# Linformer attention and maxout FFN: q's transposes of six batches moved from TensorE to the DMA crossbar, with early q loads and smaller output stores

## The chip, the cores and the metric

One core of one Trainium2 chip. The metric is device time in microseconds of one execution; most executions agree within 0.3%. Where two kernels are compared, the ratio is the mean time of one kernel's fast runs over that of the other's of the same rounds, so it is not quite the ratio of the medians quoted beside it. Executions over 1.5% slower than the fastest of the same kernel are left out of the means.

## The reference

```python
q, k, v: (8, 8, 1024, 64) f32        # batch, heads, sequence, head dim
E, F:    (64, 1024)                   # project the sequence to 64
k_proj = einsum('ks,bhsd->bhkd', E, k);  v_proj = einsum('ks,bhsd->bhkd', F, v)
attn   = softmax(q @ k_proj.T / 8) @ v_proj
x      = attn.transpose(0, 2, 1, 3).reshape(8192, 512)
h      = max(x @ w1, x @ w2, x @ w3)   # 512 -> 768
out    = h @ w_out                     # 8192 x 512 f32
```

The code calls the second half `moe`; a *chunk* is 512 tokens of it, and `jt` counts the six 128-wide blocks of the 768 hidden columns. Tokens are independent after the projections: in which order a batch's 1024 tokens pass through the scores and the FFN does not matter, as long as the stores put them back.

## The kernel before

The scores need q with the head dim on the partitions, for two heads at a time: q^T, 128 x 1024 per head pair. Before, q is loaded with tokens on the partitions, two heads are copied side by side (`q_p2`), TensorE transposes 8 blocks of 128x128 against an identity into PSUM, and a copy brings the result to SBUF. A batch has four head pairs.

```python
# in attention(b, pending), after the loads of q, k, v and the k projection
for g in range(NPAIR):                                    # 4 head pairs
    q_p2 = small.tile([P, SI, 2 * D], BF16, name="q_p2", bufs=3)
    peng = nc.vector if (b == 0 or g < 2) else nc.gpsimd
    peng.tensor_copy(out=..., in_=q_t[:, 2 * g:2 * g + 2, :, :]...)          # L135
    qt_ps = ps_s.tile([P, 512], FP32, name="ps_s").bitcast(BF16)
    for si in range(SI):                                  # 8
        nc.tensor.transpose(out=qt_ps[:, si * P:(si + 1) * P],               # L141
                            in_=q_p2[:, si, :], identity=ident)
    qT_sb = small.tile([P, SI, P], BF16, name="qT_sb", bufs=2)
    nc.any.tensor_copy(out=qT_sb, in_=qt_ps...)                              # L147
    for c in range(NCHUNK):                               # 2: scores, exp
        nc.tensor.matmul(out=sc_ps, lhsT=kpT_bd[:, g, :], rhs=qT_sb[:, csl, :], ...)  # L154
        nc.scalar.activation(out=pT_g[:, csl, :], in_=sc_ps, func=AF.Exp, scale=scale)
# ... v projection L172, attention outputs L200, x transposes L220 ...

def moe_chunk(b, xT, ch):                                 # 512 tokens
    o_acc = moe_sb.tile([P, SI_PER_CHUNK, DO], FP32, name="o_acc", bufs=2)
    for jt in range(NJT):                                 # 6
        # 12 matmuls L237 into three ps_m buffers, copy by ACT L245, two max by DVE L247, L248
    for tt in range(SI_PER_CHUNK):                        # 4
        # 6 matmuls L252 into ps_m
        nc.scalar.copy(out=o_acc[:, tt, :], in_=o_ps)                        # L259
    nc.sync.dma_start(out=ov[...], in_=o_acc)             # one store of 1 MB

for b in range(B):
    xTs[b] = attention(b, pending)
    if b == 0: load_weights()
    for args in pending: moe_chunk(*args)                 # the two chunks of batch b-1
    pending = [(b, xTs[b], ch) for ch in range(NCHUNK)]
```

A scheduler orders each engine's instructions when the kernel is built, by program order as the priority and its own estimate of times. On the chip every engine then works through its list in that order: an instruction that waits holds back all behind it on its engine or queue (at 41.57 us VectorE had stood 3.81 us behind one q copy whose load had not landed, with batch 0's outputs behind it).

The softmax here doesn't subtract the row's maximum and nothing guards it: scores larger than these inputs give would overflow.

## Time and profile before

| | before |
|---|---|
| time, median of 4 runs | 467.26 us |
| span of the profiled execution | 465.8 us |
| PE busy, of the span | 93% |
| steady batch (first k projection to the next) | 52.87 us, PE busy in all of it |
| last matmul to the end of the span | 5.36 us |

PE is TensorE, DVE VectorE, ACT ScalarE, POOL GpSimd; SP is the engine that issues the stores and transposes, and SPq its queue. In a line of a timeline come start and length in us, engine, line of the kernel, operation, out<-in and count; in brackets, the idle time before it and what ended that. A "steady batch" here is the attention of batch b woven with the first MoE chunk of batch b-1, then the second chunk alone.

### The profile page before, as it was taken

Reading aid. Unit: us, or ns where it says so; the run is one execution under the profiler, and the core shown is the slowest. Engines: PE = TensorE matmul, PEld = TensorE weight load, DVE = VectorE, ACT = ScalarE, POOL = GpSimd, SP = SyncE. Lnnn points to the kernel's source line nnn. Section 1 sums busy time; section 2 is a strip of 40 time slices with the busy share of each in tenths; the row PEclk is TensorE's granted clock in tenths of the full one; section 3 lists DMA queues with packets and bytes.
Section 4 is the critical chain, followed back from the end, with each engine's and each line's share of the span. In section 5 each row is a group of like instructions: output and inputs, shape, how many; then the busy total and the mean of one; then the engine's idle time right before and its main releaser. Section 6 shows DMA issues by size and latency. Waiting matters only on the chain.

```text
span 465.8 us, 6716 instructions
## 1 busy us (share of the span) xinstructions
PE 434.5 (93%) x2672; PEld 226.5 (49%) x2672; DVE 229.0 (49%) x550; ACT 173.6 (37%) x311; POOL 54.8 (12%) x74
## 2 busy tenths in 40 slices
PE   1474999999999999999999999999999999999995
PEld 1343555455544565455544555445544555444442
DVE  2025575427934376426935377425935277334351
ACT  1142555235432453235432553335432453322322
POOL 7212340004000320005000320001000000000000
PEclk9996999999999999999999999999999999999999
DMA  8999999319720591209820492202020200202102
GB/s 110 207 210 205 206 207 206 117 61 182 121 91 0 139 201 25 90 28 198 137 91 0 128 193 44 91 0 91 2 91 0 91 1 0 92 0 91 54 37 90
DMA packets 30207, 45.78 MB, mean 98 GB/s; under 512 B 1120, under 2 KB 28000, under 8 KB 28128
## 3 DMA queue, kind: packets, MB, share of 16 engines
q0 software_dynamic: 27872, 28.58, 38.1%
q1 hardware_dynamic: 2304, 16.78, 8.7%
q8 instruction: 21, 0.34, 0.3%
q14 instruction: 10, 0.08, 0.0%
HBM read 57.15 MB, written 16.78 MB: 159 GB/s over the span
## 4 chain that ended last, share of the span: by engine, by line
PE 89%; DMA 8%; POOL 1%; DVE 0%; issue 0%; ACT 0%; POOLq 0%
PE ps_m L237 54%; PE ps_m L252 18%; DMA q_t<-in_q_dram 6%; PE ps_s L220 3%; PE ps_s L154 3%; PE ps_s L200 3%; PE ps_s L141 3%; PE ps_s L108 3%; DMA k_t<-in_k_dram 2%; PE ps_s L172 2%; PE ps_s L120 0%; POOL q_t L101 0%; DVE x_sb L210 0%; DVE zinv L209 0%; POOL e_sb L61 0%
## 5 line engine op out<-in xcount | busy, mean ns | idle before, releaser
L237 PE MATMUL ps_m<-xT,w_sb 128*128 128x512 bf16 x1152 | 269.3, 380 | 0.0
L237 PEld LDWEIGHTS <-w_sb 128*128 128x128 bf16 x1152 | 107.6, 98 | 111.5 <-issue 3.1
L247 DVE TENSOR_TENSOR m<-ps_m,h1s 128x512 f32<-128x512 f32 x96 | 66.2, 689 | 112.6 <-PE ps_m L237 112.0
L245 ACT COPY h1s<-ps_m 128x512 f32<-128x512 f32 x96 | 56.3, 587 | 105.0 <-PE ps_m L237 104.1
L252 PE MATMUL ps_m<-wout_sb,hT 128*128 128x512 bf16 x384 | 85.7, 379 | 0.0
L248 DVE TENSOR_TENSOR hT<-ps_m,m 128x512 bf16<-128x512 f32 x96 | 66.0, 688 | 8.0 <-PE ps_m L237 2.0
L259 ACT COPY o_acc<-ps_m 128x512 f32<-128x512 f32 x64 | 37.5, 586 | 71.3 <-PE ps_m L252 71.2
L252 PEld LDWEIGHTS <-hT 128*128 128x128 bf16 x384 | 37.4, 98 | 45.1 <-DVE hT L248 3.5
L225 ACT COPY xT<-ps_s 128x512 bf16<-128x512 bf16 x58 | 34.1, 588 | 60.7 <-PE ps_s L220 60.7
L210 DVE TENSOR_TENSOR x_sb<-ps_s,zinv 128x256 bf16<-128x256 f32 x128 | 48.6, 417 | 0.2
L160 ACT ACTIVATE pT_g<-ps_s 128x512 bf16<-128x512 f32 x64 | 34.8, 596 | 19.9 <-PE ps_s L154 19.9
L220 PE MATMUL ps_s<-ident,x_sb 128*128 128x128 bf16 x256 | 35.1, 225 | 6.3 <-DVE x_sb L210 6.3
L220 PEld LDWEIGHTS <-x_sb 128*128 128x128 bf16 x256 | 21.6, 99 | 25.6 <-DVE x_sb L210 14.2
L101 POOL DMA_DIRECT2D k_t<-in_k_dram x16 | 12.0, 752 | 165.7 <-PE ps_s L108 162.1
L200 PE MATMUL ps_s<-vp_bd,pT_g 128*128 128x130 bf16 x256 | 30.3, 227 | 0.5 <-DVE vp_bd L185 0.5
L147 DVE COPY qT_sb<-ps_s 128x1024 bf16<-128x1024 bf16 x31 | 21.4, 692 | 17.4 <-PE ps_s L141 17.2
L135 POOL COPY q_p<-q_t 128x1024 bf16<-128x1024 bf16 x14 | 14.6, 1042 | 127.2 <-PE ps_s L141 110.2
L108 PE MATMUL ps_s<-k_t,eT 128*64 128x256 bf16 x128 | 17.5, 292 | 10.6 <-DMA k_t<-in_k_dram 10.6
L154 PE MATMUL ps_s<-qT_sb,kpT_bd 128*128 128x512 bf16 x64 | 20.9, 409 | 3.5 <-DVE qT_sb L147 2.4
L128 DVE COPY kpT_bd<-ps_s 64x256 bf16<-64x256 bf16 x6 | 1.7, 284 | 45.2 <-PE ps_s L120 45.2
L209 DVE RECIPROCAL zinv<-ps_s 128x4 f32<-128x4 f32 x128 | 17.8, 171 | 8.0 <-PE ps_s L200 7.8
L141 PE MATMUL ps_s<-ident,q_p 128*128 128x128 bf16 x256 | 21.3, 231 | 0.0
(39 smaller groups left out, 150.1 us busy)
## 6 DMA issues: line engine op xcount, KB each, us to landing
out_dram<-o_acc SPq DMA_DIRECT2D x16, 1024.0 KB, 3.9
q_t<-in_q_dram POOLq DMA_DIRECT2D x16, 512.0 KB, 11.4
k_t<-in_k_dram POOLq DMA_DIRECT2D x16, 512.0 KB, 8.8
v_t<-in_v_dram POOLq DMA_DIRECT2D x16, 512.0 KB, 10.7
w_sb<-in_moe_w_dram POOLq DMA_DIRECT2D x3, 768.0 KB, 22.6
wout_sb<-in_moe_w_out_dram POOLq DMA_DIRECT2D x1, 768.0 KB, 25.7
e_sb<-in_E_dram POOLq DMA_DIRECT2D x1, 128.0 KB, 3.0
f_sb<-in_F_dram POOLq DMA_DIRECT2D x1, 128.0 KB, 3.0
```

What stands on the lines that cost most here:

```text
L141: nc.tensor.transpose(out=qt_ps[:, si * P:(si + 1) * P], in_=q_p2[:, si, :], identity=ident,)
L154: nc.tensor.matmul(out=sc_ps, lhsT=kpT_bd[:, g, :], rhs=qT_sb[:, csl, :], start=True, stop=True,)
L160: nc.scalar.activation(out=pT_g[:, csl, :], in_=sc_ps, func=AF.Exp, scale=scale,)
L200: nc.tensor.matmul(out=av_v[:, gg, 0:2 * D + 2], lhsT=pT[g][:, si, :], rhs=vp_bd[:, g, :], start=(gg == 0), stop=(gg == 1),)
L210: nc.vector.tensor_tensor(out=x_sb[:, 4 * u:4 * (u + 1), :].rearrange("p (g par) d -> p g par d", par=2), in0=av_b[:, :, :, 0:D], in1=zinv ...
L220: nc.tensor.transpose(out=xt_v[:, ct, 0:P], in_=x_flat[:, ct * P:(ct + 1) * P], identity=ident,)
L237: nc.tensor.matmul(out=h_ps[i], lhsT=w_sb[i][:, ct, jt * P:(jt + 1) * P], rhs=rhs_x[:, ct, :, :], start=(ct == 0), stop=(ct == NCT - 1),)
L245: nc.scalar.copy(out=h1s, in_=h_ps[0])
L247: nc.vector.tensor_tensor(out=m12, in0=h_ps[1], in1=h1s, op=ALU.max)
L248: nc.vector.tensor_tensor(out=hT[:, jt, :], in0=h_ps[2], in1=m12, op=ALU.max)
L252: nc.tensor.matmul(out=o_ps, lhsT=hT[:, jt, tt * P:(tt + 1) * P], rhs=wout_sb[:, jt, :], start=(jt == 0), stop=(jt == NJT - 1),)
L259: nc.scalar.copy(out=o_acc[:, tt, :], in_=o_ps)
```

## The change

Intent: let the DMA engines transpose q for batches 2 to 7, so that TensorE does only products. q is loaded a batch ahead; its head-pair copies are written to a scratch in HBM, and a transposing DMA reads them back. This also puts tokens in natural order, and the output goes in 128-row stores of 256 KB. The pool of `xT` shrinks from 8 buffers to 6. A *gate* makes the copies for batch b wait for a max in the second MoE chunk of batch b-2. Cut to its core:

```diff
+    PE_BATCHES = {0, 1}                 # these keep the TensorE path
+    def q_prep(b, q_t):
+        for g in range(NPAIR):
+            q_p2 = small.tile([P, SI, 2 * D], BF16, name="q_p2", bufs=4)
+            peng = nc.vector if (g % 2 == 0) else nc.gpsimd
+            cp = peng.tensor_copy(out=..., in_=q_t[...])                       # L106
+            if b - 2 in gate: tc.add_manual_dep(cp.ins, gate[b - 2].ins.name, ...)
+            nc.sync.dma_start(out=qp_dram[b, g]..., in_=q_p2)                   # L115
+            qT = small.tile([P, S], BF16, name="qT", bufs=2 * NPAIR)
+            nc.sync.dma_start(out=qT, in_=qp_dram[b, g], transpose=True)        # L120
   def attention(b, qTs):
-    (loads q, k, v; transposes q on TensorE)
+    (loads k, v; if b in PE_BATCHES: as before, else takes qTs[g])
   def moe_chunk(b, xT, ch):
+            if ch == 1 and jt == 0: gate[b] = hmax
-        (one 1 MB store from o_acc, bufs=2)
+            o_sb = moe_sb.tile([P, DO], FP32, name="o_sb", bufs=3)
+            nc.scalar.copy(out=o_sb, in_=o_ps)                                  # L291
+            nc.sync.dma_start(out=rows, in_=o_sb)      # 128 rows, 256 KB       # L296
   for b in range(B):
     xTs[b] = attention(b, qTs[b])
     if b == 0: load_weights()
+    if b + 1 < B: q_next = q_load(b + 1)
     for args in pending: moe_chunk(*args)
+    if b + 1 < B and b + 1 not in PE_BATCHES: qTs[b + 1] = q_prep(b + 1, q_next)
```

Line numbers change: L141 becomes L171, L147 L177, L154 L185, L108 L137, L237 L266, L252 L283, L259 L291.

More of the change, by code (lines that the diff above doesn't have):

```diff
@@ L45 @@
     NCHUNK = S // CHUNK
-    SI_PER_CHUNK = SI // NCHUNK
+    NTT = S // P
     scale = 1.0 / float(D) ** 0.5
     const = ctx.enter_context(tc.tile_pool(name="const", bufs=1))
-    xt_pool = ctx.enter_context(tc.tile_pool(name="xt_pool", bufs=B))
+    xt_pool = ctx.enter_context(tc.tile_pool(name="xt_pool", bufs=6))
     work = ctx.enter_context(tc.tile_pool(name="work", bufs=2))
@@ L57 @@
     ps_m = ctx.enter_context(tc.tile_pool(name="ps_m", bufs=3, space=bass.MemoryType.PSUM))
+    qp_dram = nc.dram_tensor("qp_scratch", [B, NPAIR, S, 2 * D], BF16, kind="Internal").ap()
     e_sb = const.tile([KP, S], BF16, name="e_sb")
@@ L86, in load_weights, with q_load, attention @@
         nc.gpsimd.dma_start(out=wout_sb, in_=moe_w_out.rearrange("(jt p) m -> p jt m", p=P))
-    out_v = out.rearrange("(b p si) m -> b si p m", p=P, si=SI)
-    def attention(b, pending):
-        def drain(n=1):
-            for _ in range(min(n, len(pending))):
-                moe_chunk(*pending.pop(0))
+    PE_BATCHES = {0, 1}
+    gate = {}
+    def q_load(b):
+        q_t = work.tile([P, H, SI, D], BF16, name="q_t")
+        sv = q[b].rearrange("h (p si) d -> p h si d", si=SI)
+        for hh in range(2):
+            hs = slice(hh * (H // 2), (hh + 1) * (H // 2))
+            nc.gpsimd.dma_start(out=q_t[:, hs], in_=sv[:, hs])
+        return q_t
+    def q_prep(b, q_t):
+        qTs = []
+        for g in range(NPAIR):
+            q_p2 = small.tile([P, SI, 2 * D], BF16, name="q_p2", bufs=4)
+            peng = nc.vector if (g % 2 == 0) else nc.gpsimd
+            cp = peng.tensor_copy(
+                out=q_p2.rearrange("p si (h d) -> p si h d", h=2),
+                in_=q_t[:, 2 * g:2 * g + 2, :, :].rearrange("p h si d -> p si h d"),
+            )
+            if b - 2 in gate:
+                tc.add_manual_dep(
+                    cp.ins, gate[b - 2].ins.name,
+                    mybir.DependencyInfo(mybir.DependencyClass.Sync, mybir.DependencyReason.DATA),
+                    reason="hold q prep")
+            nc.sync.dma_start(
+                out=qp_dram[b, g].rearrange("(p si) c -> p si c", si=SI),
+                in_=q_p2,
+            )
+            qT = small.tile([P, S], BF16, name="qT", bufs=2 * NPAIR)
+            nc.sync.dma_start(out=qT, in_=qp_dram[b, g], transpose=True)
+            qTs.append(qT)
+        return qTs
+    def attention(b, qTs):
         k_t = work.tile([P, H, SI, D], BF16, name="k_t")
         v_t = work.tile([P, H, SI, D], BF16, name="v_t")
-        q_t = work.tile([P, H, SI, D], BF16, name="q_t")
-        for src, dst in ((q[b], q_t), (k[b], k_t), (v[b], v_t)):
+        for src, dst in ((k[b], k_t), (v[b], v_t)):
             sv = src.rearrange("h (p si) d -> p h si d", si=SI)
@@ L132, in attention @@
         for g in range(NPAIR):
-            q_p2 = small.tile([P, SI, 2 * D], BF16, name="q_p2", bufs=3)
-            peng = nc.vector if (b == 0 or g < 2) else nc.gpsimd
-            peng.tensor_copy(
-                out=q_p2.rearrange("p si (h d) -> p si h d", h=2),
-                in_=q_t[:, 2 * g:2 * g + 2, :, :].rearrange("p h si d -> p si h d"),
-            )
-            qt_ps = ps_s.tile([P, 512], FP32, name="ps_s").bitcast(BF16)
-            for si in range(SI):
-                nc.tensor.transpose(
-                    out=qt_ps[:, si * P:(si + 1) * P],
-                    in_=q_p2[:, si, :],
-                    identity=ident,
-                )
-            qT_sb = small.tile([P, SI, P], BF16, name="qT_sb", bufs=2)
-            nc.any.tensor_copy(out=qT_sb, in_=qt_ps.rearrange("a (si p) -> a si p", p=P))
-            pT_g = small.tile([P, SI, P], BF16, name="pT_g", bufs=5)
+            if b in PE_BATCHES:
+                q_p2 = small.tile([P, SI, 2 * D], BF16, name="q_p2", bufs=4)
+                peng = nc.vector if (b == 0 or g < 2) else nc.gpsimd
+                peng.tensor_copy(
+                    out=q_p2.rearrange("p si (h d) -> p si h d", h=2),
+                    in_=qTs[:, 2 * g:2 * g + 2, :, :].rearrange("p h si d -> p si h d"),
+                )
+                qt_ps = ps_s.tile([P, 512], FP32, name="ps_s").bitcast(BF16)
+                for si in range(SI):
+                    nc.tensor.transpose(
+                        out=qt_ps[:, si * P:(si + 1) * P],
+                        in_=q_p2[:, si, :],
+                        identity=ident,
+                    )
+                qT_g = small.tile([P, S], BF16, name="qT", bufs=2 * NPAIR)
+                nc.any.tensor_copy(out=qT_g, in_=qt_ps)
+            else:
+                qT_g = qTs[g]
+            pT_g = small.tile([P, S], BF16, name="pT_g", bufs=5)
             pT.append(pT_g)
@@ L152, in attention @@
                 sc_ps = ps_s.tile([P, 512], FP32, name="ps_s")
-                csl = slice(c * SI_PER_CHUNK, (c + 1) * SI_PER_CHUNK)
+                csl = slice(c * CHUNK, (c + 1) * CHUNK)
                 nc.tensor.matmul(
@@ L156, in attention @@
                     lhsT=kpT_bd[:, g, :],
-                    rhs=qT_sb[:, csl, :],
+                    rhs=qT_g[:, csl],
                     start=True, stop=True,
@@ L160, in attention @@
                 nc.scalar.activation(
-                    out=pT_g[:, csl, :],
+                    out=pT_g[:, csl],
                     in_=sc_ps,
@@ L190, in attention @@
         nc.vector.memset(vp_bd[KP:2 * KP, :, 2 * D + 1:2 * D + 2], 1.0)
-        xT = xt_pool.tile([P, NCT, SI, P], BF16, name="xT")
-        for si in range(SI):
+        xT = xt_pool.tile([P, NCT, S], BF16, name="xT")
+        for tt in range(NTT):
             x_sb = small.tile([P, H, D], BF16, name="x_sb", bufs=3)
@@ L201, in attention @@
                         out=av_v[:, gg, 0:2 * D + 2],
-                        lhsT=pT[g][:, si, :],
+                        lhsT=pT[g][:, tt * P:(tt + 1) * P],
                         rhs=vp_bd[:, g, :],
@@ L224, in attention @@
                 )
-            nc.any.tensor_copy(out=xT[:, :, si, :], in_=xt_v[:, :, 0:P])
+            nc.any.tensor_copy(out=xT[:, :, tt * P:(tt + 1) * P], in_=xt_v[:, :, 0:P])
         return xT
     def moe_chunk(b, xT, ch):
-        if True:
-            o_acc = moe_sb.tile([P, SI_PER_CHUNK, DO], FP32, name="o_acc", bufs=2)
-            hT = moe_sb.tile([P, NJT, CHUNK], BF16, name="hT")
-            rhs_x = xT[:, :, ch * SI_PER_CHUNK:(ch + 1) * SI_PER_CHUNK, :]
-            for jt in range(NJT):
-                h_ps = [ps_m.tile([P, CHUNK], FP32, name="ps_m") for _ in range(3)]
-                for i in range(3):
-                    for ct in range(NCT):
-                        nc.tensor.matmul(
-                            out=h_ps[i],
-                            lhsT=w_sb[i][:, ct, jt * P:(jt + 1) * P],
-                            rhs=rhs_x[:, ct, :, :],
-                            start=(ct == 0),
-                            stop=(ct == NCT - 1),
-                        )
-                h1s = moe_sb.tile([P, CHUNK], FP32, name="h1s", bufs=2)
-                nc.scalar.copy(out=h1s, in_=h_ps[0])
-                m12 = moe_sb.tile([P, CHUNK], FP32, name="m12")
-                nc.vector.tensor_tensor(out=m12, in0=h_ps[1], in1=h1s, op=ALU.max)
-                nc.vector.tensor_tensor(out=hT[:, jt, :], in0=h_ps[2], in1=m12, op=ALU.max)
-            for tt in range(SI_PER_CHUNK):
-                o_ps = ps_m.tile([P, DO], FP32, name="ps_m")
-                for jt in range(NJT):
-                    nc.tensor.matmul(
-                        out=o_ps,
-                        lhsT=hT[:, jt, tt * P:(tt + 1) * P],
-                        rhs=wout_sb[:, jt, :],
-                        start=(jt == 0),
-                        stop=(jt == NJT - 1),
-                    )
-                nc.scalar.copy(out=o_acc[:, tt, :], in_=o_ps)
-            ov = out[b * S:(b + 1) * S, :].rearrange("(p si) m -> p si m", si=SI)
-            nc.sync.dma_start(out=ov[:, ch * SI_PER_CHUNK:(ch + 1) * SI_PER_CHUNK, :], in_=o_acc)
@@ new lines, in moe_chunk @@
+        hT = moe_sb.tile([P, NJT, CHUNK], BF16, name="hT")
+        rhs_x = xT[:, :, ch * CHUNK:(ch + 1) * CHUNK]
+        for jt in range(NJT):
+            h_ps = [ps_m.tile([P, CHUNK], FP32, name="ps_m") for _ in range(3)]
+            for i in range(3):
+                for ct in range(NCT):
+                    nc.tensor.matmul(
+                        out=h_ps[i],
+                        lhsT=w_sb[i][:, ct, jt * P:(jt + 1) * P],
+                        rhs=rhs_x[:, ct, :],
+                        start=(ct == 0),
+                        stop=(ct == NCT - 1),
+                    )
+            h1s = moe_sb.tile([P, CHUNK], FP32, name="h1s", bufs=2)
+            nc.scalar.copy(out=h1s, in_=h_ps[0])
+            m12 = moe_sb.tile([P, CHUNK], FP32, name="m12")
+            nc.vector.tensor_tensor(out=m12, in0=h_ps[1], in1=h1s, op=ALU.max)
+            hmax = nc.vector.tensor_tensor(out=hT[:, jt, :], in0=h_ps[2], in1=m12, op=ALU.max)
+            if ch == 1 and jt == 0:
+                gate[b] = hmax
@@ new lines, in moe_chunk @@
+        for tt in range(CHUNK // P):
+            o_ps = ps_m.tile([P, DO], FP32, name="ps_m")
+            for jt in range(NJT):
+                nc.tensor.matmul(
+                    out=o_ps,
+                    lhsT=hT[:, jt, tt * P:(tt + 1) * P],
+                    rhs=wout_sb[:, jt, :],
+                    start=(jt == 0),
+                    stop=(jt == NJT - 1),
+                )
+            o_sb = moe_sb.tile([P, DO], FP32, name="o_sb", bufs=3)
+            nc.scalar.copy(out=o_sb, in_=o_ps)
+            r0 = b * S + ch * CHUNK + tt * P
+            rows = out[r0:r0 + P, :]
+            if b in PE_BATCHES:
+                rows = out[b * S:(b + 1) * S, :].rearrange("(p si) m -> p si m", si=SI)[:, ch * (CHUNK // P) + tt, :]
+            nc.sync.dma_start(out=rows, in_=o_sb)
@@ L263 @@
+    q_next = q_load(0)
+    qTs = {}
     pending = []
@@ L265 @@
     for b in range(B):
-        xTs[b] = attention(b, pending)
+        if b in PE_BATCHES:
+            qTs[b] = q_next
+        xTs[b] = attention(b, qTs[b])
         if b == 0:
             load_weights()
+        if b + 1 < B:
+            q_next = q_load(b + 1)
         for args in pending:
             moe_chunk(*args)
+        if b + 1 < B and b + 1 not in PE_BATCHES:
+            qTs[b + 1] = q_prep(b + 1, q_next)
         pending = [(b, xTs[b], ch) for ch in range(NCHUNK)]
```

## The prediction

> **What bounds the kernel now.** I read the head of the page first, to see whether one engine is full.
>
> ```profile
> span 465.8 us, 6716 instructions
> PE 434.5 (93%) x2672; PEld 226.5 (49%) x2672; DVE 229.0 (49%) x550; ACT 173.6 (37%) x311; POOL 54.8 (12%) x74
> PE   1474999999999999999999999999999999999995
> DMA  8999999319720591209820492202020200202102
> ```
>
> TensorE is busy 93% of the span. In slices of 11.6 us it is full from the fifth on; before that the DMA engines are full instead. Busy time of pipelined matmuls can flatter, so the chain that ended last comes next:
>
> ```profile
> PE 89%; DMA 8%; POOL 1%; DVE 0%; issue 0%; ACT 0%; POOLq 0%
> PE ps_m L237 54%; PE ps_m L252 18%; DMA q_t<-in_q_dram 6%; PE ps_s L220 3%; PE ps_s L154 3%; PE ps_s L200 3%; PE ps_s L141 3%; PE ps_s L108 3%; DMA k_t<-in_k_dram 2%; PE ps_s L172 2%; PE ps_s L120 0%; POOL q_t L101 0%; DVE x_sb L210 0%; DVE zinv L209 0%; POOL e_sb L61 0%
> ```
>
> The reader is to see two stages: a start on DMA (8%, some 37 us), then nothing but TensorE, with ACT and DVE at nearly none. In the second stage the end moves by exactly the time that is taken out of TensorE's stream. L141, which the change removes for six batches of eight, has 3% of the chain. The view by stretches, cut at the first L108 matmul of each batch, shows how regular this stage is:
>
> ```profile
> 207.49:260.36 52.87, 52.87 (x333) 27.52 (x334) 28.58 (x69) 21.05 (x38) 6.48 (x8) 1.00 0.48 100
> 260.36:313.23 52.87, 52.87 (x333) 27.51 (x334) 28.58 (x69) 21.05 (x38) 6.48 (x8) 1.00 0.48 100
> ```
>
> Columns: length, then PE, PEld, DVE, ACT and POOL busy, granted clock, DMA share, GB/s. A batch takes 52.87 us, PE is busy in all of it at full clock, and the next fullest engine, DVE, has 28.6. What a group of transposes takes of it is read from start to start in PE's timeline, because the modelled ends overlap the next group:
>
> ```profile
> 263.34 0.62 PE L141 MATMUL ps_s<-ident,q_p 128*128 128x128 bf16 x8
> 263.80 1.03 PE L237 MATMUL ps_m<-xT,w_sb 128*128 128x512 bf16 x4
> ...
> 265.17 0.61 PE L141 MATMUL ps_s<-ident,q_p 128*128 128x128 bf16 x8
> 265.62 1.03 PE L237 MATMUL ps_m<-xT,w_sb 128*128 128x512 bf16 x4
> ```
>
> Eight transposes hold the stream for 0.46 and 0.45 us, not for the 0.62 printed as their span; that is 57 ns each.
>
> **What the Trainium skill says.** (1) "TensorE: Matmul & The Clock Gate", section "Wait — 56ns, not 53.3ns?", gives 55.6 ns start to start for warm matmuls of 128 columns; the trace's 57 ns agrees, so the 231 ns mean that the group's row shows for one transpose is latency and must not be multiplied. (2) "DMA: Bandwidth & Descriptors", section "Latency and other measured facts", has 261 GB/s for DMA transposes in one kernel. The trace of before has none, so nothing here confirms it. (3) "VectorE: DVE Perf Modes", section "The three transpose paths", has 1309 ns for one 128x128 through the DMA crossbar; also not shown here. (4) "DMA: Bandwidth & Descriptors", section "Two DMAs through the same engine are not ordered": a DMA that reads what another wrote must wait for its semaphore. So each transposing read waits for its scratch write to land, on SP's queue, which also carries the output stores.
>
> **The change part by part.** *Removed from TensorE:* for batches 2 to 7, 4 groups of 8 transposes. In the batch from 260.36 the groups hold 0.46 + 0.45 + 0.45 + 0.45 = 1.81 us. The chain agrees: L141's share is 2.8% in the longer answer, 13.0 us, and only batches 1 to 7 have it on the chain, so 1.86 us each. Six batches by 1.81 are 10.9 us, all on the path. Their weight loads go with them and lie beside other work.
>
> *Removed from DVE:* 24 copies from PSUM of 0.69 us (row L147: 692 ns), 16.6 us, none of it on the path; five PSUM buffers are also asked for less often. I count nothing.
>
> *Moved:* the head-pair copies of q (0.43 us on DVE, 1.04 us on POOL) go from the attention to the second MoE chunk of an earlier batch, behind the gate. There DVE has 1.10 us idle before each max of the six (its wait rows show 1.10 after hT and before m), and two copies of 0.43 fit. The MoE psum buffers also have slack: hT of one jt ends near 295.83 and its buffer is wanted again at about 296.67. I count 0.
>
> *Added on DMA:* per batch 4 writes of 256 KB to scratch and 4 transposing reads of 256 KB. When do they run, and is there room?
>
> ```profile
> 277.00:281.00 4.00, 4.00 (x37) 2.38 (x35) 3.56 (x14) 1.72 (x3) 0.00 (x0) 1.00 1.25 209
> 285.00:289.00 4.00, 4.00 (x23) 1.95 (x22) 2.74 (x7) 0.92 (x2) 0.00 (x0) 1.00 0.00 0
> 293.00:297.00 4.00, 4.00 (x20) 1.86 (x19) 1.45 (x3) 1.30 (x3) 0.00 (x0) 1.00 0.63 262
> 301.00:305.00 4.00, 4.00 (x20) 1.84 (x19) 1.69 (x4) 1.17 (x2) 0.00 (x0) 1.00 0.00 0
> ```
>
> Same columns. Loads fill the DMA engines until about 282 us; the second chunk (292.35 to 313) leaves them empty apart from one store. The gate (hT of its first jt) would open at about 295.8. Copies end near 298, a write takes about 3 us (estimate: 256 KB against the 3.0 us that a 128 KB load and the 3.9 us that a 1 MB store took to land). A transpose at the skill's 261 GB/s is 1.0 us plus a like latency, about 3 us; four behind each other end near 311 at the latest, and the first near 304. The first score matmul of the next batch came 4.4 us after the batch's start (264.74 against 260.36), so at about 317.6. So the chain is hidden, with 13 us to spare for the first pair. The stores of a chunk come only from 309.4 on, by which time SP should be past its waits. Added on the path: 0.
>
> *Stores:* 64 of 256 KB in place of 16 of 1 MB. Only the last one is on the path.
>
> ```profile
> 460.45 0.59 ACT L259 COPY o_acc<-ps_m 128x512 f32<-128x512 f32 x1 [0.71 <-PE ps_m L252]
> 461.06 0.33 SPq L261 DMA_DIRECT2D out_dram<-o_acc  x1
> ```
>
> From this issue to the end of the span are 4.7 us. In the stretch 293 to 297 one store of 1 MB took 0.63 x 4 = 2.5 us of all 16 engines; a quarter of the bytes takes 0.6, so up to 1.9 us less. I take 1.6. Within a chunk, tiles come 1.30 us apart and there are three output buffers, so the fourth copy wants the first store landed 3 x 1.30 - 0.59 = 3.3 us after it was issued: barely enough for a 256 KB store, and a miss would cost ACT a few tenths that the three MoE psum buffers take up. I count 0.
>
> *Start:* batches 0 and 1 keep the TensorE path and nearly the same order of loads (q, k, v, weights, q, k, v), so the first 46 us should stay. There is one trap in it: DVE stood 3.81 us behind a q copy of batch 1 that waited for its load (41.57 us), with batch 0's outputs behind it. If the new program order shifts that copy, the start moves by up to 4 us either way. I count 0.
>
> *Sum:* 467.26 - 10.9 - 1.6 = 454.8 us, 2.7% less.
>
> **Rivals.** *A: SP becomes the wait.* SP serves its queue in order. If a transpose waits for its write while finished output tiles queue behind it, three output buffers fill, ACT stops in its copy, the MoE psum buffers stay held and TensorE stops. For it: the crossbar figure of 1309 ns for 128x128; eight in a row would be 10.5 us per pair (estimate from that page), 42 us per batch, past both the stores and the next batch's scores; with the queue blocked I would expect 2 to 10 us lost per batch, 465 to 500 us in all. Against it: the gate stands just behind the first chunk's stores and 13 us ahead of the second chunk's, and DMA is empty there. Also, the q load that comes free with the copies may run beside the chain and slow it. *B: the transposes were filler.* If TensorE waits on exp or DVE in the attention once the transposes are gone, part of the 10.9 us comes back as gaps. For it: DVE is nearly full in 273 to 285 (3.56 of 4). Against it: PE stands full there with MoE matmuls woven in, which the scheduler can weave in again, and DVE loses work. Time 457 to 462. *C: the start improves.* If batch 0's outputs no longer stand behind the q copy, another 3 to 4 us go: about 451. *D: only the tail or nothing comes,* since the chain moves to some other bound: unlikely, the next engine has 28.6 of 52.87 us.
>
> **Range and chances.** The step of 10.9 us is well measured; what can spoil it is A and B. I give the plain sum or C about 0.7, B or a mild A (1 to 2 us per batch) 0.24, a strong A 0.06. 2% is 457.9 us, only 3 us from the sum. Range 450.5 to 460.
>
> **What would show it right or wrong.** Right: PE records fall by 192 to about 2480; L141 has 64; a steady batch takes 51.1 us in place of 52.87 with PE busy in all of it; L147 copies fall from 32 to 8; the chain stays on PE after the start; the last store lands in about 2 to 2.5 us; transposes land in 3 us or so and the first score matmul waits for none. Wrong if: the waits show PE behind the transposing DMA or ps_m behind ACT behind a store (A); idle PE between score matmuls and L200 (B); the start of the first MoE matmul moves from 46.3 us (C or its opposite).

## The result, and the profile after

455.32 us median of 8 runs (454.07 to 456.37) against 467.27: ratio 0.9744, interval 0.9732 to 0.9755. The forecast was 454.8 us.

The head of the page and the chain of the changed kernel:

```profile
span 453.7 us, 6523 instructions
PE 423.2 (93%) x2480; PEld 216.5 (48%) x2480; DVE 218.7 (48%) x527; ACT 172.5 (38%) x310; POOL 57.4 (13%) x74
PE 87%; DMA 10%; POOL 1%; issue 1%; ACT 1%; DVE 0%; ACTq 0%; POOLq 0%
```

PE has exactly 192 matmuls fewer; its share of span and chain hardly moves, since it was the bound and still is. The steady batch, in the view by stretches (length, then PE, PEld, DVE, ACT, POOL busy, clock, DMA share, GB/s):

```profile
205.04:255.94 50.90, 50.90 (x302) 25.82 (x302) 26.79 (x65) 21.09 (x38) 6.91 (x8) 1.00 0.70 141
255.94:306.84 50.90, 50.90 (x302) 25.82 (x302) 26.79 (x65) 21.09 (x38) 5.43 (x6) 1.00 0.59 131
```

50.90 us in place of 52.87, full again, while the DMA share went from 0.48 to 0.59 and 0.70. PE's timeline shows what took the transposes' place:

```profile
258.71 0.29 PE L149 MATMUL ps_s<-ident,kp_sb 64*128 64x64 bf16 x4
258.93 1.04 PE L266 MATMUL ps_m<-xT,w_sb 128*128 128x512 bf16 x4
259.85 1.47 PE L185 MATMUL ps_s<-qT,kpT_bd 128*128 128x512 bf16 x6
```

Six score matmuls follow each other from 259.85 and none waits for a transpose; before, they came in pairs with a group of eight transposes between pairs.

Adding PE's time from start to start over one batch (260.36 to 313.23 before, 255.94 to 306.84 after) gives where the 1.98 us come from: the q transposes 1.81 to 0; the eight score matmuls 1.83 to 1.73, perhaps since one train of six enters and leaves MoE work less often than four pairs, which no run isolates; the rest, 0.07, is spread over other lines.

What the other steps look like after, in the table of DMA issues (KB each, median us from issue to landing):

```profile
out_dram<-o_sb SPq DMA_DIRECT2D x64, 256.0 KB, 2.0
qp_scratch<-q_p SPq DMA_DIRECT2D x24, 256.0 KB, 2.1
qT<-qp_scratch SPq DMA_TRANSPOSE x24, 5.4
```

And where SP spends its time, in the timeline of the DMA-issuing queue of the changed kernel:

```profile
239.04 2.40 SPq L115 DMA_DIRECT2D qp_scratch<-q_p  x4
241.54 11.55 SPq L120 DMA_TRANSPOSE qT<-qp_scratch  x4
253.15 34.00 SPq L296 DMA_DIRECT2D out_dram<-o_sb  x8
289.94 2.41 SPq L115 DMA_DIRECT2D qp_scratch<-q_p  x4
292.44 6.32 SPq L120 DMA_TRANSPOSE qT<-qp_scratch  x4
```

Four transposes hold SP for 11.55 us in one batch and 6.32 us in a later one. Between the gate and the chunk's first finished tile are some 14 us. The quicker chain fits; the slower one frees SP 0.4 us late here (at 253.09, for a tile copied by 252.69), 1.0 and 0.8 us late in the chains of batches 3 and 4, and then the fourth output copy waits 1.0 to 1.5 us for a buffer. TensorE waits for none of this in batches 3 to 5.

At the start it does wait. Near 80 us batch loads still fill the DMA engines, and near 101 us the first four transposes, which held SP for 12.72 us, free it 1.8 us after the first tile was copied (timeline of the changed kernel):

```profile
77.45 6.49 SPq L296 DMA_DIRECT2D out_dram<-o_sb  x4
...
82.99 0.59 ACT L291 COPY o_sb<-ps_m 128x512 f32<-128x512 f32 x1 [2.98 <-DMA out_dram<-o_sb]
...
83.63 13.97 PE L266 MATMUL ps_m<-xT,w_sb 128*128 128x512 bf16 x64 [1.22 <-ACT o_sb L291]
...
104.95 0.59 ACT L291 COPY o_sb<-ps_m 128x512 f32<-128x512 f32 x1 [2.84 <-DMA out_dram<-o_sb]
...
106.07 0.29 PE L149 MATMUL ps_s<-ident,kp_sb 64*128 64x64 bf16 x4 [0.45 <-ACT kp_sb L145]
```

The fourth output copy waits 2.98 us for a buffer that a store still reads, ACT holds a MoE PSUM buffer that long, and TensorE stands for 1.22 us. In the next chunk the fourth copy waits 2.84 us, the copy `kp_sb` of batch 2 stands behind it on ACT, and TensorE stands for 0.45 us.

The whole difference of the spans, by stretch:

| stretch | before, us | after, us | difference |
|---|---|---|---|
| to the first k projection of batch 1 | 50.30 | 49.96 | -0.3 |
| batch 1, with both chunks of batch 0 | 51.4 | 52.8 | +1.4 |
| batch 2 | 52.9 | 51.4 | -1.5 |
| batches 3 to 6 | 211.49 | 203.59 | -7.9 |
| batch 7 and its MoE, to the last matmul | 94.34 | 92.35 | -2.0 |
| last matmul to the end | 5.36 | 3.61 | -1.8 |
| sum | 465.8 | 453.7 | -12.1 |

### The profile page after: what moved, and what is told of

It is laid out like the page before. It is cut to its first block, busy times and chain, and to the rows that moved or that the text cites.

```text
span 453.7 us, 6523 instructions
## 1 busy us (share of the span) xinstructions
PE 423.2 (93%) x2480; PEld 216.5 (48%) x2480; DVE 218.7 (48%) x527; ACT 172.5 (38%) x310; POOL 57.4 (13%) x74
## 4 chain that ended last, share of the span: by engine, by line
PE 87%; DMA 10%; POOL 1%; issue 1%; ACT 1%; DVE 0%; ACTq 0%; POOLq 0%
PE ps_m L266 55%; PE ps_m L283 17%; DMA q_t<-in_q_dram 5%; PE ps_s L251 3%; PE ps_s L231 3%; PE ps_s L185 3%; PE ps_s L137 2%; DMA k_t<-in_k_dram 2%; PE ps_s L203 2%; DMA out_dram<-o_sb 2%; PE ps_s L171 0%; ACT o_sb L291 0%; PE ps_s L149 0%; POOL q_t L98 0%; DVE x_sb L241 0%
## 5 line engine op out<-in xcount | busy, mean ns | idle before, releaser
L266 PE MATMUL ps_m<-xT,w_sb 128*128 128x512 bf16 x1152 | 269.8, 380 | 1.2 <-ACT o_sb L291 1.2
L266 PEld LDWEIGHTS <-w_sb 128*128 128x128 bf16 x1152 | 108.0, 98 | 117.5 <-issue 6.9
L283 PE MATMUL ps_m<-wout_sb,hT 128*128 128x512 bf16 x384 | 85.7, 379 | 0.0
L291 ACT COPY o_sb<-ps_m 128x512 f32<-128x512 f32 x64 | 37.5, 586 | 77.3 <-PE ps_m L283 67.5
L256 ACT COPY xT<-ps_s 128x512 bf16<-128x512 bf16 x64 | 37.6, 588 | 58.1 <-PE ps_s L251 58.1
L283 PEld LDWEIGHTS <-hT 128*128 128x128 bf16 x384 | 37.5, 98 | 44.9 <-DVE hT L277 3.2
L191 ACT ACTIVATE pT_g<-ps_s 128x512 bf16<-128x512 f32 x64 | 32.8, 617 | 10.7 <-PE ps_s L185 10.7
L106 POOL COPY q_p<-q_t 128x1024 bf16<-128x1024 bf16 x12 | 14.8, 1261 | 164.6 <-DVE hT L277 164.6
L251 PEld LDWEIGHTS <-x_sb 128*128 128x128 bf16 x256 | 21.5, 100 | 26.3 <-DVE x_sb L241 13.2
L137 PE MATMUL ps_s<-k_t,eT 128*64 128x256 bf16 x128 | 17.5, 292 | 10.7 <-DMA k_t<-in_k_dram 10.7
L185 PE MATMUL ps_s<-qT,kpT_bd 128*128 128x512 bf16 x64 | 19.8, 409 | 3.1 <-DVE qT L177 3.1
L137 PEld LDWEIGHTS <-eT 128*64 128x64 bf16 x128 | 14.2, 116 | 14.2 <-issue 13.4
L231 PEld LDWEIGHTS <-pT_g 128*128 128x128 bf16 x256 | 19.7, 101 | 2.7 <-DVE vp_bd L216 1.2
```

The source lines that it names most:

```text
L137: nc.tensor.matmul(out=kp_ps[0:KP, hh * (H // 2) * D:(hh + 1) * (H // 2) * D], lhsT=eT[:, si, :], rhs=k_t[:, hs, si, :], start=(hh == 0 an ...
L185: nc.tensor.matmul(out=sc_ps, lhsT=kpT_bd[:, g, :], rhs=qT_g[:, csl], start=True, stop=True,)
L231: nc.tensor.matmul(out=av_v[:, gg, 0:2 * D + 2], lhsT=pT[g][:, tt * P:(tt + 1) * P], rhs=vp_bd[:, g, :], start=(gg == 0), stop=(gg == 1),)
L251: nc.tensor.transpose(out=xt_v[:, ct, 0:P], in_=x_flat[:, ct * P:(ct + 1) * P], identity=ident,)
L256: nc.any.tensor_copy(out=xT[:, :, tt * P:(tt + 1) * P], in_=xt_v[:, :, 0:P])
L266: nc.tensor.matmul(out=h_ps[i], lhsT=w_sb[i][:, ct, jt * P:(jt + 1) * P], rhs=rhs_x[:, ct, :], start=(ct == 0), stop=(ct == NCT - 1),)
```

## Experiments

Theory: the gain is the time that 192 transposes held TensorE's stream, plus a shorter last store, and it exists only because the DMA chain is hidden between the gate and the next scores. Rivals: the new program order or early load brought it; or the chain was never close to mattering.

### 1. The stores alone

```diff
 (kernel before)
-    one 1 MB store per chunk from o_acc, bufs=2
+    four 256 KB stores per chunk from o_sb, bufs=3
```

> The kernel before, with only the stores changed: 64 of 256 KB from three buffers in place of 16 of 1 MB from two. My theory (transposes and tail are separate terms): the tail shrinks by 1.75 us as it did in the changed kernel (5.36 to 3.61 us from the last matmul to the end), and the stores of the first chunk, which meet the loads still in flight near 80 us, cost TensorE about 1.2 us as they did there: 466.7 us, within 0.3% of the kernel before. Rival (the stores are part of the gain in the steady stage): 1 us or more per 50 us batch gone, 460 us or less. Transposes stay, so the steady batch should stay at 52.9 us.

Measured: 466.39 us against 467.01, ratio 0.9988 (0.9976 to 1.0). Both halves of the theory hold: from the last matmul to the end 3.6 us, and PE waits 1.2 us once for ACT behind a store. The steady batch stays at 52.9 us. The stores are worth about 0.6 us net, with an interval that reaches 0, and have nothing to do with the steady gain.

### 2. All of the change but the DMA transposes

```diff
-    PE_BATCHES = {0, 1}
+    PE_BATCHES = set(range(B))
```

> The changed kernel with all eight batches on the TensorE path: small stores, early q load and pool sizes stay, the DMA transposes are gone. If the transposes on TensorE are the whole steady gain: the steady batch goes back to 52.9 us from 50.9 and the time to 455.3 + 6 x 1.98 = 467.2 us or a little less. Rival (the early q load or the new program order gives part of the gain): clearly under 465 us with a steady batch between 51 and 52.5 us.

Measured: 467.42 us against 467.01, ratio 1.0005 (0.9995 to 1.0014). Two starts of a batch in the chain of this run:

```profile
209.08 1.93 PE ps_s L137 x16
262.02 1.86 PE ps_s L137 x16
```

52.9 us apart, as before. So early load, order and pool sizes bring nothing by themselves, and putting q on the DMA is worth 12 us: the rival falls.

### 3. Each transpose twice

```diff
 (kernel before)
-            for si in range(SI):
+            for si in [i for i in range(SI) for _ in range(1 if b < 2 else 2)]:
                 nc.tensor.transpose(...)
```

> The kernel before with each q transpose of batches 2 to 7 done twice into the same place: 192 transposes more, the result stays right. If a transpose costs TensorE's stream its start-to-start time of 57 ns: 467.3 + 192 x 0.057 = 478.2 us, 1.81 us more per steady batch. If it costs the 231 ns that its row shows: 511 us. If the seventeen hundredths per batch that the change gained beyond 1.81 us are the cost of entering and leaving a group (which doubling does not add), this run shows 1.81 and not 1.98 per batch.

Measured: 480.2 us, 13.2 more than the kernel before where 10.9 were expected. In PE's timeline of this run:

```profile
271.89 1.05 PE L141 MATMUL ps_s<-ident,q_p 128*128 128x128 bf16 x16
272.78 1.24 PE L237 MATMUL ps_m<-xT,w_sb 128*128 128x512 bf16 x5
...
276.68 0.59 PE L154 MATMUL ps_s<-qT_sb,kpT_bd 128*128 128x512 bf16 x2 [0.29 <-ACT qT_sb L147]
```

Sixteen transposes hold the stream for 0.89 us, 56 ns each, so the start-to-start price holds and the 231 ns of the row (511 us) is out. The surplus is a side effect of my edit: the build put most copies from PSUM on another engine. The groups by form show 25 of 32 on ACT:

```profile
L147 ACT COPY qT_sb<-ps_s 128x1024 bf16<-128x1024 bf16 x25 | 25.3, 1012 | 2.7 <-PE ps_s L141 1.7
```

At 1012 ns in place of DVE's 692 the scores wait for one of them, 0.29 us in each of batches 2 to 7. The batch took 55.1 us, 2.24 more than before, of which the transposes explain about 1.8 and this wait 0.29. On the 0.17 us per batch beyond 1.81 the run is inconclusive for this reason.

### 4. Six output buffers

```diff
-            o_sb = moe_sb.tile([P, DO], FP32, name="o_sb", bufs=3)
+            o_sb = moe_sb.tile([P, DO], FP32, name="o_sb", bufs=6)
```

> The changed kernel with six output buffers in place of three, nothing else; the order of instructions on every engine is the same. Theory (rival A of the prediction came true once or twice, mildly): TensorE's idle 1.2 us at 83.6 us, when ACT waited for an output buffer while stores shared the DMA engines with loads, and about 0.4 us at the next chunk go: 453.7 us (1.2 to 1.7 us less). Rival (the stall is hidden by later slack, or moves to another wait): no change, under 0.4 us.

Measured: 453.46 us, ratio to the kernel before 0.9706 (0.9683 to 0.9729), so some 1.9 us under the changed kernel. The same place in its timeline:

```profile
79.58 6.64 PE L266 MATMUL ps_m<-xT,w_sb 128*128 128x512 bf16 x29
79.78 0.59 ACT L291 COPY o_sb<-ps_m 128x512 f32<-128x512 f32 x1 [0.71 <-PE ps_m L283]
```

The fourth copy runs 1.3 us after the third and PE goes straight on. Batch 1 takes 51.4 us again (49.02 to 100.39, from k projection to k projection) and batch 2 takes 50.90 (to 151.29), a full steady batch. Both stalls were on the path.

### 5. No gate

```diff
-            if b - 2 in gate:
+            if False:
```

> The changed kernel without the gate. The scheduler then puts the q copies of all later batches into DVE's and POOL's queues early (next to batch 1's attention and the first MoE chunk of batch 0), though their loads land much later. Theory: the gate is what keeps them from blocking; without it DVE stands in its queue for loads of later batches, MoE results and PSUM buffers wait, TensorE idles in the first 150 us: 470 us or more, worse than the kernel before. Rival (the copies are ready anyway and the order is only another order): 455 us, within 1 us.

Measured: 508.21 us, ratio 1.0875. From the timeline of this run, SP, ACT and PE:

```profile
101.53 4.47 SPq L120 DMA_TRANSPOSE qT<-qp_scratch  x2
...
119.16 2.08 SPq L296 DMA_DIRECT2D out_dram<-o_sb  x3
...
127.88 0.58 ACT L291 COPY o_sb<-ps_m 128x512 f32<-128x512 f32 x1 [33.67 <-DMA out_dram<-o_sb]
128.52 12.77 PE L266 MATMUL ps_m<-xT,w_sb 128*128 128x512 bf16 x47 [31.91 <-ACT o_sb L291]
```

Without the gate the built order puts writes and transposes of later batches ahead of the first stores. Their loads have not landed, SP stands, finished tiles find no buffer, and TensorE idles 31.9 us in one piece. I had put the block on DVE. DVE's q copies did stand there, 54 us between 60 and 160 us, for loads and for buffers that scratch writes held, and PE waited 13 us behind DVE, in four waits. But the 31.9 us came through SP's queue and the output buffers, which is rival A of the prediction.

### 6. The gate five jt later

```diff
-            if ch == 1 and jt == 0:
+            if ch == 1 and jt == NJT - 1:
```

> The changed kernel with the gate at the sixth (last) jt of the chunk, 12.95 us later. In the changed kernel the chain from gate to the last issue of a transpose takes 9.3 us (289.4 to 298.8) and the first score matmul comes 21.3 us after the gate (310.75), so with 13 us less some 8 us are left for the first pair's copy, write and transpose (about 6 to 9 us) and the stores of the chunk lie in the same stretch. Theory (hidden with room, but with no more than about 13 us): TensorE starts to wait for a transpose or behind a store, 0.5 to 2 us per batch, 458 to 467 us. Rival (it is hidden whatever the gate): 455 us. Rival A at full strength: over 475 us.

Measured: 518.49 us, ratio 1.1098. Rival A at full strength, where I had expected 0.5 to 2 us per batch: the scores wait 52.8 us for transposes, in 13 waits. One batch of this run, from the timelines of SP and PE:

```profile
302.02 1.49 SPq L120 DMA_TRANSPOSE qT<-qp_scratch  x1
303.56 3.78 SPq L115 DMA_DIRECT2D qp_scratch<-q_p  x2
317.98 2.50 SPq L120 DMA_TRANSPOSE qT<-qp_scratch  x2
...
316.58 1.03 PE L185 MATMUL ps_s<-qT,kpT_bd 128*128 128x512 bf16 x2 [8.53 <-DMA qT<-qp_scratch]
```

The second transpose, issued from 302.02, serves the scores only at 316.58. Two things were wrong in my estimate. The build also interleaved writes and transposes with stores on SP, and the last two pairs' transposes stand there 10 us for the landing of their writes. And q's and k's loads of later batches were issued at 298.6 and 302.4, so writes and transposes ran beside them. In the last prepared batch, where no load is issued any more, the last two transposes start at 370.44, 3 us after the writes (367.47). During the waits the clock falls to 0.5, which makes the loss larger: from 318 to 320 us, still at 0.5, PE does 7 matmuls where it did 11 from 298 to 300. What of the 63 us is order and what is load, this run does not separate. It shows that the chain is hidden by its place, not by being cheap.

### 7. The early q load held until the transposes have landed

```diff
             ld = nc.gpsimd.dma_start(out=q_t[:, hs], in_=sv[:, hs])
+            if b - 2 in last_t:           # last transposing read of batch b-2
+                tc.add_manual_dep(ld.ins, last_t[b - 2].ins.name, ...)
```

> The changed kernel with each early q load held until the last transposing read of the scratch (two batches before it) has landed. In the changed kernel four transposes take 11.6 to 12.7 us of SP's issue where a q load runs beside them (batches 2 to 5) and 5.2 to 6.3 us where none does (6 and 7). If the load beside them is the cause: 5 to 6.5 us in every batch here, and since the chain is hidden either way the time stays within 1 us of the changed kernel's 455.3 (perhaps 0.4 us less, where SP's block held the first store of batch 0's second chunk back). If the transposes of the early batches are slow for another reason: 11 us or more remain.

Measured: four transposes hold SP for 5.2 to 6.3 us in batches 2 to 6, so the load beside them was what made it 11.6 to 12.7. But the time was 469.4 us, ratio 1.0057: the whole gain was gone, which I had not expected. The timeline of this run shows where:

```profile
251.69 5.24 SPq L126 DMA_TRANSPOSE qT<-qp_scratch  x4
262.85 8.17 SPq L302 DMA_DIRECT2D out_dram<-o_sb  x4
270.07 0.59 ACT L297 COPY o_sb<-ps_m 128x512 f32<-128x512 f32 x1 [4.66 <-DMA out_dram<-o_sb]
```

The held load now runs beside the second chunk's stores. With three output buffers the fourth copy waits 4.66 us, and PE waits after it: 1.9 to 2.8 us for `kp_sb`, which stands behind that copy on ACT, in each of batches 2 to 5, 9.3 us in all. The clock is down around it (0.79, 0.50 and 0.85 in the three slices from 270 to 276 us), which costs more: four MoE matmuls hold PE 1.68 us from 271.51, against 0.92 us at 258.93 in the changed kernel. The chain of waits has a store of 6.7 to 7.7 us in each of these batches. In the changed kernel the load collides with the transposes, whose lateness the buffers still absorb in batches 3 to 5; here with the stores, where they do not. Six buffers together with this hold were not run.

### 8. Batch 1 on the DMA path too

```diff
-    PE_BATCHES = {0, 1}
+    PE_BATCHES = {0}
```

> The changed kernel with batch 1 on the DMA path as well, without a gate for it. If each batch moved brings its 1.98 us: 453.3 us. Rival (batch 1's q lands only at about 41 us and the scratch write and transposing read share the DMA engines with k and v of batch 1, so the scores at 54.7 us wait, and POOL's copies stand in front of loads): slower than the changed kernel by 1 to 8 us, 456 to 463 us.

Measured: 482.41 us, ratio 1.0315: the rival, 27 us over the changed kernel where it said 1 to 8. TensorE's timeline has four waits for transposes at the scores of batch 1, the longest:

```profile
69.32 1.04 PE L185 MATMUL ps_s<-qT,kpT_bd 128*128 128x512 bf16 x2 [8.81 <-DMA qT<-qp_scratch]
```

All loads of batches 1 and 2 run then, and three transposes hold SP for 21.95 us. POOL's copies also stand between k's loads and delay one by 20 us. The start is the wrong place for the DMA path as built here; batch 1 has to stay in `PE_BATCHES` (batch 0 was not tried).

### 9. Batch 1's q copies on POOL

```diff
-                peng = nc.vector if (b == 0 or g < 2) else nc.gpsimd
+                peng = nc.vector if b == 0 else nc.gpsimd
```

> The changed kernel with batch 1's q copies all on POOL; PE's, ACT's and SP's orders stay the same. Theory of the start (rival C): DVE no longer stands 3.4 us behind the copy that waits for q's load, so batch 0's outputs and the first MoE matmul (45.5 us) come 3 to 4 us earlier and the time falls to about 452. Rival (the start is bound by the loads: in PE's order the k projection of batch 1, at 50.0 us, stands behind only nine MoE matmuls, and its k lands at about 49): the first MoE matmul comes earlier, but the k projection still waits for its load, and the time falls by 1 us or less, to 454.3 or more.

Measured: 453.48 us, ratio 0.9701 (0.9674 to 0.9727), some 1.9 us under the changed kernel. From PE's timeline of the changed kernel:

```profile
45.55 1.49 PE L266 MATMUL ps_m<-xT,w_sb 128*128 128x512 bf16 x3
49.96 0.41 PE L137 MATMUL ps_s<-k_t,eT 128*64 128x256 bf16 x2
```

and of this run:

```profile
37.30 0.63 PE L266 MATMUL ps_m<-xT,w_sb 128*128 128x512 bf16 x1
46.18 0.38 PE L137 MATMUL ps_s<-k_t,eT 128*64 128x256 bf16 x2 [4.41 <-DMA k_t<-in_k_dram]
```

The first MoE matmul comes 8 us earlier, yet the time falls by 1.9 us only: nine MoE matmuls later PE's order has the k projection, and that waits 4.41 us for its load. It still starts 3.8 us earlier than in the changed kernel, but its second half waits 0.58 us more, and batch 2 begins only 0.8 us earlier. Both theories were half right; the loads take back most. (The profiled run, 454.75 us, was the slowest of the five.)

### 10. Both repairs

```diff
 experiment 4's edit and experiment 9's edit
```

> The changed kernel with both small repairs, six output buffers and batch 1's q copies on POOL. Their gains lie in different stretches (83 to 107 us, and before 53 us), so they should add: 455.3 - 1.8 - 1.8 = 451.7 us. Rival (one of the two waits was only hidden behind the other): 453.3 us as each alone.

Measured: 452.11 us (451.66 to 453.99), ratio 0.9692 (0.9673 to 0.9711). The gains lie close to a sum (451.7 expected). This is the fastest version found: 0.5% under the changed kernel by the two ratios, which come from different rounds.

### 11 and 12. More work for TensorE at the start

```diff
 (experiment 10)
     for b in range(B):
+        if b == 1: moe_chunk(*pending.pop(0))     # 11 and 12
         xTs[b] = attention(b, qTs[b])
     load order of batch 0: q, k, v  ->  k, q, v   # 12 only
```

> Both repairs, and the first MoE chunk of batch 0 is put ahead of batch 1's attention in program order, so that TensorE has work while batch 1's k is still loading. In the run with POOL copies it idled 4.4 + 0.6 us for that load (41.8 to 46.2 us and once more) after the first MoE matmul at 37.3 us. If MoE work fills this: 451.7 - 4 to 5 = 447 us. Rival (the attention of batch 1 then lacks MoE matmuls to weave in, and its waits on exp and DVE come out): 450 us or more.

> As the run with the first chunk ahead of batch 1's attention, and batch 0's k is loaded before its q. TensorE's first k projection waits for k's load (15.7 us, 10 us of idle); with k first it starts about 5 us earlier, near 10.5 us, and the rest of batch 0's attention, which is a chain of waits, follows. If this chain sets the first MoE matmul: 3 to 4 us less again, 443 to 444 us. Rival (q, which is needed right after, or the weights, which land near 31 us, set it): under 1.5 us less.

Measured: 457.44 us (451.77 to 461.51, six runs) and 457.22 us (456.45 to 457.47). Two of the first one's six runs, 460.21 and 461.51, count as slow; the four fast ones lie between 451.77 and 457.91, ratio 0.9743 (0.9698 to 0.9787), which still overlaps experiment 10's interval, so that one is not shown to be slower. The second is, at 0.9792 (0.9779 to 0.9805). Both miss the gain that I expected. In the traces the start did gain: batch 2 begins at 98.54 us in the first (whose profiled run, 457.91, is the slowest of the fast ones) and at 92.27 us in the second, against 99.81 us in experiment 10. But batch 3 begins at 156.15 and 155.68 us in them and at 150.71 us in experiment 10. Between lies the first DMA chain. In the first of the two runs SP has:

```profile
79.53 14.47 SPq L120 DMA_TRANSPOSE qT<-qp_scratch  x3
94.09 0.53 SPq L115 DMA_DIRECT2D qp_scratch<-q_p  x1
101.45 1.17 SPq L120 DMA_TRANSPOSE qT<-qp_scratch  x1
```

Here the build put the fourth write behind three transposes, loads run beside them, and the scores of batch 2 wait for the last transpose (4.5 us in the list of waits; 9.4 us in experiment 12), after which the clock is at 0.5 again (108 to 112 us in the first). Why the first of the two varies from run to run, over 6 us among its fast runs alone, stays open.

## Why the prediction was right

- **The bound.** Right: PE full in the steady batch before and after, and a batch shorter by what was removed.
- **10.9 us from the transposes.** Right in kind and nearly in size: 56 to 57 ns from start to start. The six batches gave 11.4 us (1.5 + 7.9 + 2.0 in the table of stretches). Per batch, 1.98 in place of 1.81: the score matmuls, which now run in trains, take 0.10 less, and 0.07 is spread over other lines. Batch 2 gave only 1.5, because TensorE stood 0.45 us behind an output copy; with six buffers it gave the full 1.98.
- **1.6 us from the last store.** 1.8 us; a 256 KB store landed in 2.0 us by the median.
- **DMA chain hidden.** Right in result, with a thinner margin than told. A transpose landed in 5.4 us by the median, where I had taken 3; the 3 is nearly right only without loads (3.3 us at least, 3.7 by the median in experiment 7). The 261 GB/s that I took were not reached: with the last batch's transposes alone (346 to 350 us) the DMA engines, at a share of 0.90 to 1.15, moved 190 to 195 GB/s. My "near 311" was also a wrong sum: 304 us and three more of 3 us are 313. I had named the q load beside the chain as a danger; experiment 7 shows that this was the difference. My 13 us of slack were for the first pair. That SP would be past its waits when the stores come was wrong for the chunks whose chain ran beside a load: it came free 0.4 to 1.8 us late, and the three buffers took that up everywhere but in batch 2.
- **Moved copies count 0.** Right in result. But a copy on DVE took 845 ns by its row and not 430 with POOL copying at the same time, and POOL's 1261 and not 1042; the buffers' slack took it up.
- **Output buffers "barely enough".** The one miss of sign: the store near 80 us shared the DMA engines with loads, the one near 101 us went out late, and the step "I count 0" was worth about 1.4 us in batch 1 and 0.45 us in batch 2. Experiment 4 got both back. I had judged a store's time in a quiet stretch.
- **Start unchanged.** Right (-0.3 us). That 3.8 us of DVE blocking were at stake there was too much: experiment 9 took the block away and got 1.9, because the k load came next.
- **Rivals.** A's mechanism is real and stood close by: with the gate absent or elsewhere the time is 53 or 63 us over the changed kernel. B (gaps in place of transposes) fell: PE has no gap in a steady batch. C did not come by itself, and D fell.
- **The sum.** That 454.8 lies 0.5 us from the measured 455.32 is partly luck: the output buffers' 1.4 us in batch 1 were nearly made up by 0.5 us more from the transposes, 0.2 from the tail and 0.3 at the start.

## What to carry to other kernels

On a full TensorE, price an instruction from start to start and multiply; a row's mean duration was four times too much here. When work is moved to the DMA engines, its own time matters less than its place: find the stretch between two bursts of the same queue, pin the work there, and then ask what each transfer that comes free will run beside. Holding one transfer to protect another may only move the collision: in experiment 7 it cost the whole gain.

## What the Trainium skill lacked or had wrong

- "Advanced Engine Details and Errata", section "X-Bar Transpose (TRN2)", says that transpose DMAs are as fast as regular ones. Here a plain write of 256 KB landed in 2.1 us and a transposing read of the same bytes in 5.4 us by the median, 3.3 at best, 11.8 at worst; four held SP's queue for 5.2 to 6.3 us alone and 11.6 to 12.7 us beside a load. Landing times include the wait behind earlier transposes; but alone, from 346 to 350 us, transposes moved 190 to 195 GB/s, against 383 in the microsecond from 343, which was mostly writes.
- "VectorE: DVE Perf Modes", section "The three transpose paths": 1309 ns for one 128x128 through the crossbar is no price per block in a larger transfer. A whole 128x1024, eight blocks, landed in 3.3 us at best, 0.41 us per block.
- "DMA: Bandwidth & Descriptors", section "Issuing engines are not separate DMA queues", says that DMAs of all engines interleave on the same 16 DMA engines, but has no figure for what a small store suffers beside a large load. Here a 256 KB store took 2.0 us by the median, and in experiment 7, beside a q load, 6.7 to 7.7 us of the chain.
- "SBUF — State Buffer", section "Who interferes with whom", has DVE copies in a two-port mode and GpSimd exclude each other at a shared port, and gives slowdowns only without the operations that were run. Here two copies at the same time took longer (DVE 845 ns in place of 424, POOL 1261 in place of 1041 in the changed kernel). That would fit, though no run here isolates the cause.
